# Transfers of x spaced in time, a token order of their own for the last two units, and new orders around 9-product jobs

## The chip, the cores and the metric

The kernel runs on one core of a Trainium2 chip. A core has five engines that run side by side, each its own instruction stream in order: TensorE (PE, matrix products; its weight loads are shown as PEld), VectorE (DVE), ScalarE (ACT), GpSimd (POOL) and SyncE (SP), which here issues nearly all DMA transfers. Products land in PSUM, eight banks of 128 x 512 float32 each, and have to be read out by VectorE or ScalarE before a bank can be written again. The metric is the device time of one execution in microseconds (us); the time before is the median of three runs.

## What is computed

The input x has 2048 rows of 512. Two branches are formed from it and mixed by a gate for each row:

```python
g = _sigmoid((x * gate_w).sum(-1, keepdims=True))
a = _A_ref(x, A_wq, A_wk, A_wv, A_wo)     # attention, 32 heads of 16, one shared key and value head
b = _B_ref(x, B_w_gate, B_w_up, B_w_down) # ((x W) * (x V)) W2, inner width 1792, no nonlinearity
return g * a + (1 - g) * b
```

The attention branch computes `scores = q k^T * 16^-0.5`, a softmax over the 2048 keys, and the weighted sum of the values, followed by the product with `wo`. All is float32 and stays accurate to it: a dense product of two float32 matrices is made of three products of their high and low parts (`mm3`, line 144).

## The kernel before

**Units and steps.** The queries are cut into 4 chunks `c` of 512 rows, 4 row tiles `t` of 128 in each, and 4 groups `g` of 8 heads. A unit is one (c, g, t): 64 units (line 107), each with 16 steps over the keys. For each step there are two products that give scores for the row maximum (`p1`, L705, tokens a and b, read by VectorE's maximum L706), two products that give the scores again with the maximum already subtracted (`p2`, L746, tokens c and d, read by ScalarE's exponential L747), and the products with the values (`pv`, L759; one token p is a round of 8 small products, two steps). The first kind runs 25 steps ahead (`LEAD`). When a unit's 16 steps of the first kind are done, `p1_end` (line 710) reduces the maxima, stores them to DRAM (`dm<-mt`, L726), and fetches them back as rows of the tile `Q` (`Q<-dm`, L733): the first product L746 of the unit can't start before these rows have landed.

**Lanes and fill.** The products a to f use 64 rows of the array each, and the two halves are two lanes: a, c, e on the one, b, d, f on the other; two products of different lanes run side by side. Tokens e and f are the fill: one product of 64 rows of the dense work of the FFN branch, of the projection to q and of the product with `wo` (L878). A `Job` is a chain of such products into one PSUM bank; the first lane runs 12 products ahead of the second, and when the second has done its last the bank is read out by the job's `evac`. A gate or up job has 12 products. For each group of FFN columns (`FGS`, of 3, 3, 4 and 4 columns of 128) four down jobs follow, one for each row tile, of 9 products (3 columns x 3) or 12. Four jobs of 9 fill the 36 fill tokens of exactly one unit, and such a unit has an order of its own.

**The written order.** PE's instructions stand in the order of strings of tokens: `ORDER` (144 tokens: 16 each of a to d, 36 each of e and f, 8 p) for a unit, `ORDER_NINE` for a unit with 9-product jobs, `ORDER_AFTER` for the unit behind it. The choice is made at the end of the function (line 971). There are 8 units of the second kind and 8 of the third. A planner that runs when the program is built (`State`, lines 408 to 482, and the dictionary `clock`) follows the order with assumed durations; it picks the PSUM bank for each product (`claim`), skips fill for which nothing is ready, and decides when DMA issues and the small work of the other engines are put into the streams: `later(ns, fn)` puts `fn` that many planned nanoseconds behind the present. Each stream keeps its order on the chip, so a late SP instruction holds back all that stand behind it in SP's stream.

**x.** The transposed x of a chunk, high and low part, is 8 tiles of 128 x 512 (256 KB each). At the start x of chunks 1 to 3 lies in tiles that the FFN uses later, and is stored to DRAM (`x_store`, L311: 24 transfers, planned from 35 us on, one each 1.2 us; the planner's zero lies at about 33 us of the span). When a chunk's FFN is done, `x_turn` loads the next chunk's x back (`x_load`, L198), all 8 transfers at once, and the next chunk's first job counts as ready 12 us later (`xat`).

**y.** Each output tile is the sum of five parts. `y_add` (line 350): ScalarE scales the first out of PSUM into y; for the others ScalarE scales the product out of PSUM into `yt` (L360) and GpSimd adds it (L361). Only in the tail, behind the last unit, VectorE does both in one instruction (L353). `st["idle"]` is true from the last product for the maxima (token a or b) on, about half way through the unit before the last; from there VectorE has little left to do. From there also, `claim` takes the bank that is free and was written last instead of the one that is free first, and tokens a and b serve as fill tokens.

Of the kernel before, what the change touches and what calls it, by code (L numbers as in the profile page):

```python
# [14 lines left out]
F32 = mybir.dt.float32  # L15
# [13 lines left out]
NJ = 16  # L29
# [9 lines left out]
GAP = 50.0  # L39
SEEN = 452.0  # L40
RED, RED_END = 602.0, 688.0
EXP, EXP_END = 490.0, 604.0
COPY, COPY_END = 505.0, 600.0
# [6 lines left out]
ORDER = (  # L50
    "cdefedafcfebefedafeedafcfedebefadebefcfefefebededebefadfefcfadeefebedcfa"
    "fcfcfafefefafafcfefafcfedcfafafefedebcfebefebebebcbppppcdadcbppdababcppb"
)
ORDER_NINE = (
    "cbedcefefafedafcffeadefedbeedfacfefafcfaffeebedbefcfedeebedaffcaffcfaeff"
    "faedfafcfcfeebcbcfededfebeeddappbcbcbappppbcabedeffedefecbefafefedebabpp"
)
ORDER_AFTER = (
    "adebcffefeadeebcfedebeffeadefadedaffefcfafeedbebecffeafcfaffcfedeaffcfeb"
    "cefefebabedcdpppcbcbadppcbdeebeffcebafedefedafcfefafcfebcfedefafedbapppb"  # L60
)
HALVES = (slice(0, 64), slice(64, 128))
KROWS = (slice(0, 48), slice(64, 112))
# [4 lines left out]
def mix_kernel(ctx: ExitStack, tc: tile.TileContext, x, wq, wk, wv, wo, wg, wu, wd, gw, out):  # L68
    nc = tc.nc
# [17 lines left out]
    def w512(tag, dt, bufs):  # L87
        return work.tile([128, 512], dt, name=tag, tag=tag, bufs=bufs)
# [26 lines left out]
    NS = NU * NJ  # L115
    clock = {"T": 0.0, "dve": 0.0, "act": 0.0, "pool": 0.0}
# [3 lines left out]
    def later(ns, fn):  # L120
        heapq.heappush(events, (clock["T"] + ns, next(serial), fn))
# [5 lines left out]
    def spend(eng, ns, after=0.0):  # L127
        clock[eng] = max(clock[eng], clock["T"], after) + ns
        return clock[eng]
# [29 lines left out]
    def ms_bank(i):  # L159
        return bank(i, f"ms{i}")  # L160
# [22 lines left out]
    st = {"gen": None, "next": None, "q": 0, "tail": False, "idle": False, "f": 0}  # L183

    xT = {}
    xd = {}

    def x_tiles(tags=None):
        if tags:
            return [[w512(tag, F32R, FG + 1) for _ in range(4)] for tag in tags]  # L190
        whole = [work.tile([128, 4, 512], F32R, name=tag, tag=tag, bufs=1) for tag in ("xh", "xl")]
        return [[w[:, k] for k in range(4)] for w in whole] + whole

    def x_load(c):
        xT[c] = x_tiles()
        for v in range(2):
            for k in range(4):
                nc.sync.dma_start(xT[c][v][k].bitcast(F32), xd[c][v * 4 + k])  # L198

    dq, dqat = {}, {}  # L200

    def at(t, fn):
        later(max(0.0, t - clock["T"]), fn)
# [143 lines left out]
    y = {}  # L347
    ydone = {}

    def y_add(c, t, p, gcol):  # L350
        end = spend("act", COPY)
        if st["tail"] and (c, t) in y:
            nc.vector.scalar_tensor_tensor(y[c, t], p, gcol, y[c, t], op0=OP.mult, op1=OP.add)  # L353
        elif (c, t) not in y:
            y[c, t] = w512("y", F32, 6)
            ydone[c, t] = 0
            nc.scalar.activation(y[c, t], p, AF.Copy, scale=gcol)
        else:
            tmp = w512("yt", F32, 2)
            nc.scalar.activation(tmp, p, AF.Copy, scale=gcol)  # L360
            nc.gpsimd.tensor_tensor(y[c, t], y[c, t], tmp, op=OP.add)  # L361
            end = spend("pool", 1240.0, end)
        ydone[c, t] += 1
        if ydone[c, t] == len(FGS) + 1:
            done = y.pop((c, t))
            at(end + 200.0, lambda: nc.sync.dma_start(out2[c * 512 + t * 128:c * 512 + t * 128 + 128, :], done))


    class Job:


        def __init__(self, prods, evac, ready, p=None, start=True):
            self.prods, self.evac, self.ready, self.p, self.start = prods, evac, ready, p, start
            self.end = self.items = self.bank = None
# [7 lines left out]
    def peek():  # L382
        if st["next"] is None and st["gen"] is not None:
            st["next"] = next(st["gen"], None)
            if st["next"] is None:
                st["gen"] = None
        if front and ready(front[0]) and (len(front) > 1 + (st["f"] > 9) and not st["tail"] or not ready(st["next"])):
            return front[0]
        return st["next"] if ready(st["next"]) else None

    def nine_unit():
        if nines and ready(nines[0][1][0]):
            group, group_jobs = nines.popleft()
            begun.add(group)
            nine.extend(group_jobs)
        return bool(nine)

    def take():
        if nine:
            return nine.popleft()  # L400
        j = peek()
        if front and j is front[0]:
            return front.popleft()
        st["next"] = None
        return j

    class State:
# [21 lines left out]

        def claim(self):  # L430
            b = self.free.index(min(self.free))
            if st["idle"] or self.npv == 0:
                b = max((i for i in range(NB) if self.free[i] <= max(min(self.nl), self.free[b])), key=lambda i: self.wrote[i])
            self.known = max(self.known, self.wrote[b])
            return b
# [42 lines left out]

    def evac(j, p):
        clock["act"] = max(clock["act"], clock["T"] + SEEN)  # L480
        j.evac(p)


# [7 lines left out]
    xat = {0: 0.0}  # L491
# [13 lines left out]

    def x_turn(c):
        x_load(c)
        xat[c] = clock["T"] + 12000.0

    order = [(c, f) for c in range(NC) for f in range(NF)]  # L510
    staged, W = {}, {}
# [296 lines left out]
    later(100.0, gate_sum)  # L808
    later(70000.0, gates)
    for i, f in enumerate(stores):  # L810
        later(35000.0 + 1200.0 * i, f)
    qat.update({0: 0.0, 1: 5000.0})
    st["gen"] = ffn_jobs()
    E = State()
# [10 lines left out]
    def fence():  # L825
        b = E.claim()
        p, t = bank(b, "fence"), work.tile([128, 32], F32, name="ft", bufs=2)
        for _ in range(2):
            nc.tensor.transpose(p[:32, :32], ident[:32, :32], ident[:32, :32])
            nc.vector.tensor_copy(t[0:32, :], p[:32, :32])  # L830
        E.seq += 1
        E.wrote[b] = E.known = E.seq
        E.nl = [max(E.nl) + 1000.0] * 2
        E.dve = max(E.dve, E.nl[0])
        E.free[b] = E.nl[0] + 300.0

    def fill(l):
        wait = 0.0
        if l == 0:
            if hole[0]:  # L840
                hole[0] -= 1
                run.append(None)
                pos[0] += 1
                return
            if not run or run[-1] is None or run[-1][1] + 1 == len(run[-1][0].items):
                for _ in range(40):
                    if nine or peek():
                        break
                    wait_ns(100.0)
                else:  # L850
                    hole[0] = 11
                    run.append(None)
                    pos[0] += 1
                    return
                j = take()
                j.items, j.bank = j.prods(), E.claim()
                wait, E.free[j.bank] = E.free[j.bank], 1e18
                j.p = ms_bank(j.bank)
                run.append((j, 0))
            else:  # L860
                run.append((run[-1][0], run[-1][1] + 1))
            j, i = run[-1]
        else:
            if run[pos[1]] is None:
                pos[1] += 1
                return
            j, i = run[pos[1]]
            if i == 0 and j.end > E.known:
                if E.npv:
                    late[0] += 1  # L870
                    return
                fence()
        pos[l] += 1
        at = E.issue(l, wait)
        E.wrote[j.bank] = E.seq
        lhs, rhs = j.items[i]
        end = i + 1 == len(j.items)
        nc.tensor.matmul(j.p, lhs[HALVES[l]], rhs[HALVES[l]], start=(l == 0 and i == 0), stop=(l == 1 and end))  # L878
        if end and l == 0:
            j.end = E.seq  # L880
        elif end:
            clock["T"], clock["act"] = max(clock["T"], at), max(E.act, at + SEEN)
            E.free[j.bank] = clock["act"] + COPY_END + GAP
            evac(j, j.p)
            E.act = max(E.act, clock["act"])

    def token(op):
        place(op)
        while late[0] and run[pos[1]][0].end <= E.known:
            late[0] -= 1  # L890
            fill(1)
# [32 lines left out]
    def wait_ns(ns):  # L924
        E.nl = [max(E.nl) + ns] * 2
        events_until(max(E.nl))
# [21 lines left out]
    while min(E.n1) < LEAD or pos[0] < FIRST[0] or pos[1] < FIRST[1]:  # L948
        l = 0 if E.nl[0] <= E.nl[1] else 1
        k = E.n1[l]  # L950
# [8 lines left out]
    is_nine = False  # L959
    while E.npv < NS:  # L960
        after, is_nine = is_nine, E.npv > 0 and not st["idle"] and nine_unit()
        for op in ORDER_NINE if is_nine else ORDER_AFTER if after else ORDER:
            token(op)
    events_until(max(E.nl))

# [9 lines left out]
    while events or front or st["gen"] or st["next"]:  # L975
        run_events()
        if peek():
            j = take()
# [28 lines left out]
```

## Time and profile before

| | |
|---|---|
| median of 3 runs | 1612.77 us (1607.96 to 1616.8) |
| the profiled execution: its own time | 1613.99 us |
| the profiled execution: span from first to last instruction | 1611.2 us |
| mean granted TensorE clock | 0.996 |
| PE busy | 1595.3 us, 99% |
| PE weight loads busy | 1039.4 us, 65% |
| DVE busy | 1360.5 us, 84% |
| ACT busy | 1205.8 us, 75% |
| POOL busy | 734.3 us, 46% |
| products for the maximum (L705), for the exponential (L746), with the values (L759), fill (L878) | 2048, 2048, 4096, 4752 |
| DMA | 121.44 MB, mean 75 GB/s |

The span and the run's own time differ by 2.8 us that lie outside the first and the last instruction. A busy PE is not a PE at its peak: products are pipelined, their recorded ends are modelled, and two lanes that are both busy look like one that is busy and one that is idle. So for PE the starts tell more than the busy share: how long a unit takes from one landmark in the order to the same landmark in the next. A landmark that is easy to find is the run of four rounds (`acc`, L759, x32) near the end of `ORDER`.

### The profile page before, as it was taken

How to read it: one execution, taken by the hardware profiler on the slowest of the kernel's cores; microseconds unless marked ns; L12 is line 12 of the kernel's file. 1: busy time of each engine (PE TensorE's matmuls, PEld its weight loads, DVE VectorE, ACT ScalarE, POOL GpSimd, SP SyncE). 2: the span in 40 equal slices, each digit the busy share in tenths (PEclk: the TensorE clock that was granted, in tenths of full speed). 3: DMA queues.
4: the chain of work that ended last, by engine and by line, in shares of the span. 5: the costliest groups of instructions: out<-in, count | busy, mean ns of one | idle time of the engine just before them, and what ended most of it. 6: DMA issues, size and time to landing. Idle time of an engine off the chain costs nothing.

```text
span 1611.2 us, 35399 instructions
## 1 busy us (share of the span) xinstructions
PE 1595.3 (99%) x13126; PEld 1039.4 (65%) x13126; DVE 1360.5 (84%) x2410; ACT 1205.8 (75%) x2380; POOL 734.3 (46%) x875
## 2 busy tenths in 40 slices
PE   9999999999999999999999999999999999999998
PEld 7766766665665666666666666576676666676665
DVE  6978988888988988888898888898878888888870
ACT  4667877787787777787787778787777777787785
POOL 5616636354534624454533635454442624554431
PEclk9999999999999999999999999999999999999999
DMA  5464322121232212121232212122232212221111
GB/s 162 159 212 130 98 65 70 46 69 54 67 105 77 73 48 73 55 73 54 59 110 67 76 54 74 50 70 67 61 94 65 73 54 75 59 64 52 33 30 40
DMA packets 184991, 121.44 MB, mean 75 GB/s; under 512 B 46196, under 2 KB 154356, under 8 KB 184820
## 3 DMA queue, kind: packets, MB, share of 16 engines
q1 hardware_dynamic: 183620, 118.87, 24.6%
q8 instruction: 103, 1.69, 0.4%
q14 instruction: 68, 0.56, 0.1%
q10 hardware_dynamic: 1200, 0.33, 0.1%
HBM read 82.96 MB, written 36.17 MB: 74 GB/s over the span
## 4 chain that ended last, share of the span: by engine, by line
PE 96%; DVE 1%; DMA 1%; SPq 0%; ACT 0%; issue 0%; POOL 0%; POOLq 0%; DVEq 0%
PE ms L878 32%; PE acc L759 28%; PE s L705 17%; PE s L746 17%; DVE mx L706 1%; PE ms L149 1%; DMA xl<-xd 0%; DMA Q<-dm 0%; DMA dq<-oh 0%; PE wo L149 0%; PE warm L770 0%; ACT P L747 0%; SPq L198 0%; SPq L726 0%; DMA dm<-mt 0%
## 5 line engine op out<-in xcount | busy, mean ns | idle before, releaser
L706 DVE TENSOR_REDUCE mx<-s 128x1 f32<-128x512 f32 x2048 | 1289.3, 685 | 186.9 <-PE s L705 108.6
L747 ACT ACTIVATE P<-s 128x512 f32<-128x512 f32 x2048 | 1061.5, 625 | 276.7 <-PE s L746 188.7
L746 PE MATMUL s<-Q,KK 50*128 50x512 f32 x2048 | 712.7, 410 | 7.0 <-DMA Q<-dm 6.7
L705 PE MATMUL s<-KK,Q 48*128 48x512 f32 x2048 | 708.0, 404 | 0.7 <-DMA Q<-dq 0.6
L759 PE MATMUL acc<-P,V 128*32 128x512 f32 x4096 | 479.6, 597 | 0.0
L746 PEld LDWEIGHTS s<-Q,KK 50*128 50x128 f32 x2048 | 358.7, 186 | 141.3 <-issue 53.8
L705 PEld LDWEIGHTS s<-KK,Q 48*128 48x128 f32 x2048 | 356.0, 186 | 102.6 <-issue 52.6
L878 PE MATMUL ms<-xh,wl 64*128 64x512 f32 x920 | 329.2, 393 | 0.0
L878 PE MATMUL ms<-xh,wh 64*128 64x512 f32 x920 | 326.1, 393 | 0.0
L878 PE MATMUL ms<-xl,wh 64*128 64x512 f32 x920 | 313.1, 392 | 0.0
L759 PEld LDWEIGHTS acc<-P,V 128*32 128x32 f32 x4096 | 117.9, 109 | 254.7 <-issue 223.3
L878 PEld LDWEIGHTS ms<-xh,wh 64*128 64x128 f32 x920 | 165.9, 186 | 15.1 <-issue 0.6
L361 POOL TENSOR_TENSOR y<-y,yt 128x512 f32<-128x512 f32 x63 | 81.2, 1288 | 204.6 <-ACT yt L360 204.6
L544 POOL TENSOR_TENSOR hf<-gs 128x512 f32<-128x512 f32 x56 | 72.1, 1287 | 220.7 <-ACT gs L533 220.6
L878 PEld LDWEIGHTS ms<-xh,wl 64*128 64x128 f32 x920 | 163.0, 186 | 8.7 <-issue 0.3
L878 PEld LDWEIGHTS ms<-xl,wh 64*128 64x128 f32 x920 | 156.1, 186 | 10.5
L878 PE MATMUL ms<-wdh,hl 64*128 64x512 f32 x448 | 162.6, 396 | 0.0
L878 PE MATMUL ms<-wdh,hh 64*128 64x512 f32 x448 | 162.1, 397 | 0.0
L641 POOL TENSOR_TENSOR oT<-raw,rb 128x128 f32<-128x128 f32 x63 | 28.9, 459 | 292.2 <-DMA rb<-dr 280.9
L878 PE MATMUL ms<-wdl,hh 64*128 64x512 f32 x448 | 161.1, 393 | 0.0
L137 POOL TENSOR_TENSOR wl<-wn,wh 128x512 fp32r<-128x512 f32 x116 | 149.3, 1287 | 9.3
L763 ACT COPY osb<-acc 128x512 f32<-128x512 f32 x64 | 37.5, 586 | 89.5 <-PE acc L759 83.2
(147 smaller groups left out, 1342.5 us busy)
## 6 DMA issues: line engine op xcount, KB each, us to landing
do<-osb SPq DMA_DIRECT2D x63, 256.0 KB
wn<-in_B_w_gate_dram SPq DMA_DIRECT2D x56, 256.0 KB
wn<-in_B_w_up_dram SPq DMA_DIRECT2D x56, 256.0 KB
wdn<-in_B_w_down_dram SPq DMA_DIRECT2D x56, 256.0 KB
Q<-dq SPq DMA_DIRECT2D x384, 32.0 KB
raw<-do SPq DMA_DIRECT2D x252, 32.0 KB
dq<-oh SPq DMA_DIRECT2D x16, 256.0 KB
dq<-ol SPq DMA_DIRECT2D x16, 256.0 KB
```

Of the source, the lines that this page charges most:

```text
L137: nc.gpsimd.tensor_tensor(lo, src, hi.bitcast(F32), op=OP.subtract)
L149: nc.tensor.matmul(p, l, r, start=start and i == 0, stop=stop and i == len(prods) - 1)
L361: nc.gpsimd.tensor_tensor(y[c, t], y[c, t], tmp, op=OP.add)
L544: nc.gpsimd.tensor_tensor(hf, gu[0], gu[1], op=OP.mult)
L641: nc.gpsimd.tensor_tensor(dst, raw[:, 0], rb, op=OP.mult)
L705: nc.tensor.matmul(p, q[r, slot], KK[r, kq * 512:(kq + 1) * 512], start=True, stop=True)
L706: nc.vector.tensor_reduce(mx[u][:, half * 4 + slot, kq:kq + 1], p, axis=AX.X, op=OP.max)
L746: nc.tensor.matmul(p, KK[r, j * 128:(j + 1) * 128], q[r].rearrange("p s q -> p (s q)"), start=True, stop=True)
L747: nc.scalar.activation(P[s][:, half], p, AF.Exp, scale=0.25)
L759: nc.tensor.matmul(acc[u][b:b + 32, :], V[:, j + i], src[:, half], start=(j == 0), stop=(j == NJ - 2))
L763: nc.scalar.copy(osb, acc.pop(u))
L878: nc.tensor.matmul(j.p, lhs[HALVES[l]], rhs[HALVES[l]], start=(l == 0 and i == 0), stop=(l == 1 and end))
```

## The change

It has five parts.

1. `x_load` puts its 8 transfers 2.5 us apart, and the job behind them counts as ready 23.5 us after the turn instead of 12. The 24 stores of `x_store` start at 8 us of the planner's time instead of 35, 2 us apart instead of 1.2.
2. The last two units are run from one string, `ORDER_LAST` (250 tokens: 7 each of a and b, 32 each of c and d, 72 e, 84 f, 16 p in runs of 5, 3, 3 and 5), instead of twice from `ORDER`.
3. From `st["idle"]` on, `y_add` uses VectorE's one instruction instead of ScalarE and GpSimd, and the planner counts the bank as free when VectorE is done.
4. `claim` takes the bank that is free first also after `st["idle"]`.
5. `ORDER_NINE` and `ORDER_AFTER` are new strings with the same counts of tokens. The rounds p stand in runs of 2, 2, 2, 2 in the first (2, 4, 2 before), and of 3, 2, 3 in the second (as before).

```diff
 ORDER_NINE = (
-    "cbedcefefafedafcffeadefedbeedfacfefafcfaffeebedbefcfedeebedaffcaffcfaeff"
-    "faedfafcfcfeebcbcfededfebeeddappbcbcbappppbcabedeffedefecbefafefedebabpp"
+    "cdebedefefafcbededeefebcfafcfefafcfefafbedefedafecfebefedabcffefefcfafef"
+    "afedafefcfebcfefccfebedadppadbadappadcdbappbcbeededefefcbefebcfefebabppf"
 )
 ORDER_AFTER = (
-    "adebcffefeadeebcfedebeffeadefadedaffefcfafeedbebecffeafcfaffcfedeaffcfeb"
-    "cefefebabedcdpppcbcbadppcbdeebeffcebafedefedafcfefafcfebcfedefafedbapppb"
+    "adefafcfebecffebefcebdedefaebedefafcfdefafeebedbedeafefdefedaefdebeedcfa"
+    "fcffeeffecffafefcebcfebcfafefdefafccfebfeadeffebcbapppdcbadcppbcbadapppb"
+)
+ORDER_LAST = (
+    "cdebefebefefedededebbcfefefebefedaefefefadcfefafcfefafefedadefebefedefcf"
+    "efcfafabefefedcffefcfefedccfeffcfedefcpppppdedcfefcfcfefefefedefeedcfefe"
+    "dfedcpppefedededeffefefededefedefefedcfcffcfefededdefefcfcffedfcfefefefe"
+    "fcfpppfcfcffcdfdfcfcdfffccfcfppppp"
 )
 def x_load(c):
         xT[c] = x_tiles()
-        for v in range(2):
-            for k in range(4):
-                nc.sync.dma_start(xT[c][v][k].bitcast(F32), xd[c][v * 4 + k])
+        for i in range(8):
+            later(2500.0 * i, lambda i=i: nc.sync.dma_start(xT[c][i // 4][i % 4].bitcast(F32), xd[c][i]))
 def y_add(c, t, p, gcol):
-        end = spend("act", COPY)
-        if st["tail"] and (c, t) in y:
+        end = spend("act", 0.0 if st["idle"] else COPY)
+        if st["idle"] and (c, t) in y:
+            end = spend("dve", 690.0)
             nc.vector.scalar_tensor_tensor(y[c, t], p, gcol, y[c, t], op0=OP.mult, op1=OP.add)
 def claim(self):
             b = self.free.index(min(self.free))
-            if st["idle"] or self.npv == 0:
+            if self.npv == 0:
 def evac(j, p):
         clock["act"] = max(clock["act"], clock["T"] + SEEN)
+        if st["idle"]:
+            clock["dve"] = max(clock["dve"], clock["T"] + SEEN)
 def x_turn(c):
         x_load(c)
-        xat[c] = clock["T"] + 12000.0
+        xat[c] = clock["T"] + 23500.0
     for i, f in enumerate(stores):
-        later(35000.0 + 1200.0 * i, f)
+        later(8000.0 + 2000.0 * i, f)
 def fill(l):
             evac(j, j.p)
-            E.act = max(E.act, clock["act"])
+            if st["idle"]:
+                E.free[j.bank] = max(E.dve, clock["dve"]) + 100.0 + GAP
+            E.act, E.dve = max(E.act, clock["act"]), max(E.dve, clock["dve"])
     while E.npv < NS:
         after, is_nine = is_nine, E.npv > 0 and not st["idle"] and nine_unit()
-        for op in ORDER_NINE if is_nine else ORDER_AFTER if after else ORDER:
+        last = E.npv == NS - 2 * NJ
+        for op in ORDER_LAST if last else ORDER_NINE if is_nine else ORDER_AFTER if after else ORDER:
             token(op)
```

## The prediction, made before the result was known

> **What bounds the kernel now.** The page comes first, for which engine the end hangs on.
>
> ```profile
> span 1611.2 us, 35399 instructions
> PE 1595.3 (99%) x13126; PEld 1039.4 (65%) x13126; DVE 1360.5 (84%) x2410; ACT 1205.8 (75%) x2380; POOL 734.3 (46%) x875
> ...
> PE 96%; DVE 1%; DMA 1%; SPq 0%; ACT 0%; issue 0%; POOL 0%; POOLq 0%; DVEq 0%
> ```
>
> TensorE carries 96% of the chain that ended last. All of its products stay, so only time that TensorE spends badly can be won. The busy share can't show that time (two lanes), so I read the chain in order of time for the landmark, the run of four rounds (x32) near the end of `ORDER`; the numbers are start and length in us.
>
> ```profile
> 51.00 8.38 DVE mx L706 x14
> 75.22 3.57 PE acc L759 x32
> 79.69 1.86 PE acc L759 x16
> ...
> 99.92 3.57 PE acc L759 x32
> 128.70 3.57 PE acc L759 x32
> ...
> 200.08 3.57 PE acc L759 x32
> ...
> 272.30 3.57 PE acc L759 x32
> ...
> 1132.52 3.60 PE acc L759 x32
> 1156.29 3.57 PE acc L759 x32
> ...
> 1181.91 6.21 DMA xl<-xd
> ...
> 1210.02 3.58 PE acc L759 x32
> ...
> 1377.38 3.57 PE acc L759 x32
> ...
> 1449.93 3.57 PE acc L759 x32
> ...
> 1544.97 3.57 PE acc L759 x32
> ...
> 1600.50 2.29 PE wo L149 x9
> ```
>
> A calm unit takes 1156.29 - 1132.52 = **23.77 us**. Against it stand four losses.
> - Unit 1: 99.92 - 75.22 = 24.70, **0.93** too long.
> - Unit 2: 128.70 - 99.92 = 28.78, **5.01** too long.
> - Around the last load of x: 1210.02 - 1156.29 = 53.73 for two units, **6.19** too long.
> - Each 9-product unit with the one behind it: from 200.08 to 272.30 lie three units, 72.22 against 71.31, **0.91** too long; the last of the eight such triples, 1377.38 to 1449.93, is 1.24 too long. A pair so takes about 72.22 - 23.77 = 48.45.
>
> What the first three wait for is told by the waits, SP's issues and the windows (PE, PEld, DVE, ACT and POOL busy, clock, DMA share, GB/s).
>
> ```profile
> PE s L746 <- DMA Q<-dm: 6.7, 3, 3.2
> ```
>
> ```profile
> 103.12 3.38 SPq L225 DMA_DIRECT2D Q<-dq  x6
> 106.60 2.68 SPq L726 DMA_DIRECT2D dm<-mt  x4
> ```
>
> ```profile
> 1156.62 1.29 SPq L726 DMA_DIRECT2D dm<-mt  x4
> ...
> 1158.87 0.54 SPq L733 DMA_DIRECT2D Q<-dm  x2
> ...
> 1178.69 1.76 SPq L198 DMA_DIRECT2D xh<-xd  x4
> 1180.55 1.80 SPq L198 DMA_DIRECT2D xl<-xd  x4
> 1182.39 4.15 SPq L225 DMA_DIRECT2D Q<-dq  x6
> 1187.26 2.10 SPq L726 DMA_DIRECT2D dm<-mt  x4
> ```
>
> ```profile
> 1191.05 1.62 DMA Q<-dm
> ```
>
> ```profile
> 100.00:105.00 5.00, 5.00 (x46) 1.57 (x44) 4.12 (x9) 1.59 (x4) 1.89 (x2) 1.00 0.95 311
> ```
>
> ```profile
> 1180.00:1185.00 5.00, 5.00 (x48) 1.66 (x50) 4.07 (x10) 1.51 (x3) 4.86 (x7) 1.00 0.92 302
> ...
> 1190.00:1195.00 5.00, 2.20 (x10) 2.23 (x12) 0.41 (x2) 1.40 (x3) 0.00 (x0) 0.65 0.54 161
> ```
>
> TensorE waits three times for the maxima's way through DRAM, at most 3.2 us. In a calm unit the store `dm<-mt` is issued at 1156.62; a period later that would be 1180.39, but it was issued at 1187.26, **6.87 late**, behind 8 loads of x and six fetches `Q<-dq` that themselves took 4.15 because the DMA engines were 92% busy. Unit 2 is the same with stores of x: `dm<-mt` went out at 106.60 behind fetches of 3.38, in a stretch of 95%. Its unit began 9.03 after the run at 99.92 (see 1553.97 below), at 108.95, 2.35 later; the calm store goes out 8.7 ahead of need (1156.29 + 9.0 - 1156.62). A wait of 3.2 us costs 6.19 because the granted clock falls to 0.65 behind it: the wait is half of the loss, the slow clock the other.
>
> **Part 1, transfers of x.** Nothing is removed: 24 loads and 24 stores of 256 KB remain, each an SP issue of 1.80 / 4 = 0.45. What changes is who stands behind them. At the last turn the `Q<-dq` and `dm<-mt` meet one load instead of eight: 0.45 of issue and 256 KB at the 302 GB/s of the full window, 0.87; 1.3 us. Calm slack: from 1156.62 to the end of the fetch's issue 2.8, landing 1.6 more (the chain's row at 1191.05), so 4.4 of 8.7; 4.3 are left. A store and a fetch that each meet a load use 2.6. The stall of 6.19 goes; I take **-6.1** (bounds 0 and -6.2). The job on the new x comes after four down jobs, 48 fill tokens, at 36 a unit 31.7 us, so readiness at 23.5 is hidden; the cover is 8 us. The other two turns lie in no stall and keep none by the same sum.
>
> The stores now run from 41 to 87 us of the span (33 + 8, then 46) instead of 68 to 96 and later. Unit 2 (maxima at about 100) is free of them: -5.0. Unit 1 still meets one at a time: 0.5 of its 0.93 stays. Together **-5.4** (bounds 0 and -5.9). In exchange, SP has stores ahead of unit 0's `dm<-mt` and of the fetches for units 2 and 3. Until 59.4 (51.00 + 8.38) the chain runs over VectorE's maxima, which hide a late first L746; unhidden it costs at most 2 x 1.3. I take **+0.3** (0 to +2.6), as the cover ends about when the first L746 is due.
>
> [...]
>
> **Part 5, the orders around 9-product jobs.** Slot and run lengths come from the rows.
>
> ```profile
> 1586.89 0.39 PE L878 MATMUL ms<-wdh,hh 64*128 64x512 f32 x1
> 1587.12 0.39 PE L878 MATMUL ms<-wdh,hl 64*128 64x512 f32 x1
> ```
>
> One lane starts a product each 0.23; a pair of different lanes shares a slot. A round is (3.57 - 1.86) / 2 = 0.855. `ORDER` has 136 products, 68 slots, 15.64, and 8 rounds, 6.84; what is left of 23.77, 1.29, belongs to three runs, 0.43 each. I counted slots in the strings, pairing neighbours of different lanes between runs: the old pair has 137 slots and 6 runs (31.51 + 13.68 + 2.58 = 47.77), the new one 136 slots and 7 runs (31.28 + 13.68 + 3.01 = 47.97). So the old pair's waits are 48.45 - 47.77 = 0.68, and the new string's bare length is 0.20 worse. What the waits are:
>
> ```profile
> PEld s L705 <- ACT P L747: 1.3, 4, 0.8
> PEld s L746 <- ACT P L747: 0.9, 4, 0.3
> PEld s L705 <- DVE mx L706: 0.8, 1, 0.8
> PEld s L746 <- DVE mx L706: 0.8, 1, 0.8
> ```
>
> In the window of the first pair TensorE's weight loads wait for banks that ScalarE and VectorE have still to read. If the new order frees all of it, a pair gains 0.48, eight 3.8; if none, it loses 0.20, eight +1.6. Shorter runs (2, 2, 2, 2) feed the readers more evenly, so I take half of the waits, 48.31: **-1.1** (bounds -3.8 and +1.6).
>
> **Parts 2 to 4, the last two units.**
>
> ```profile
> 1553.97 0.50 PE L705 MATMUL s<-KK,Q 48*128 48x512 f32 x1
> ```
>
> ```profile
> 1589.30 3.12 ACT L747 ACTIVATE P<-s 128x512 f32<-128x512 f32 x6
> ```
>
> ```profile
> L353 DVE SCALAR_TENSOR_TENSOR y<-wo,gg,y 128x512 f32<-128x512 f32 x1 | 0.8, 751 | 0.9 <-PE wo L149 0.9
> ```
>
> They last from 1553.97 to the last `wo` job at 1600.50, 46.53. The rows at 1586.89 and 1587.12 are successive starts of fill, 0.23 apart with the second lane empty: fill of one lane was used up early. `ORDER_LAST` has 72 e and 84 f, just what is left, 124 slots (28.52), 16 rounds (13.68) and 4 runs (1.72): 43.92. That is 2.61 less; 0.5 for waits gives **-2.1** (bounds -2.6 and +0.5). ScalarE's 64 exponentials at 3.12 / 6 = 0.52 are 33.3 of 43.9, so it can follow. The y sums that move to VectorE, at most five, cost 0.75 each on an engine that has no more maxima to take there; behind them in its stream wait only the reciprocals and the split for the last job. If that cover were gone it would be 3.8. `claim` alone I cost at nothing, since bank waits are in the 0.5.
>
> **Sum.** -6.1 - 5.4 + 0.3 - 1.1 - 2.1 = -14.4. The profiled run took 1613.99, 2.8 more than its span, so it would be 1599.6; it lies 1.2 over the median, so from the median I forecast **1598.4**.
>
> **Rivals.**
> - *The orders lose all waits.* For it: the waits are for banks alone. Against: the readers' load is unchanged. Pairs at -3.8, the last units at -2.6, unit 1 whole (-0.6 more): 1594.6.
> - *Banks hold the orders back.* ScalarE and VectorE empty banks no faster, so denser orders only move the waits: pairs +1.6, last units 0, 1603.2. For it: the four wait rows. Against: VectorE is busy 84%, ScalarE 75%. [...]
> - *The pacing doesn't pace.* SP's stream is in order; if it is held at another transfer's wait, the loads bunch again and one long stall stays: about +5, 1603.4. For it: SP took 4.15 over six fetches.
> - *Slower.* Loads of x now cover 20 us of each turn, and a unit sends maxima each 23.77 us, so nearly every turn has a `dm<-mt` among them, and so do units 0 and 1 with the stores. If one transfer ahead used up the slack, three turns would lose 6.2 each (+18.5 against the forecast) and two starts 5 each (+10): 1627. It decides where a met transfer costs over half of the 4.3 slack, 2.1; I found 1.3.
>
> **How the numbers follow.** Forecast 0.52, waits gone 0.16, banks 0.13, bunching 0.11, slower 0.04, rests 0.04. The range 1591 to 1606 holds the first four with the scatter of the runs. No change within 0.5% (about what a measurement of this kernel can tell) means over 1604.7: faster 0.83 (the first three and part of the fourth), same 0.13, slower 0.04.
>
> **What would show it.** Right: no unit over 24.5 us, clock 1.00 around both places, the `dm<-mt` behind the last turn issued about 8 us ahead of its unit; pairs near 48.3; 44.4 from the last two units' begin to the `wo` job. Wrong: an `xd` transfer in the chain, a wait of L746 for `Q<-dm` at units 0 or 1, or pairs above 48.6.

## The result, and the profile after

The changed kernel takes **1595.85 us** (median of 4 runs, 1594.36 to 1597.38) against 1612.65 (median of 4, 1607.96 to 1616.8): a ratio of **0.9897, 95% interval 0.9868 to 0.9926**, 16.8 us. The forecast was 1598.4 with 1591 to 1606. The profiled execution took 1595.37 us with a span of 1593.6, 17.6 less than before.

First the page of the changed kernel, then its chain of work in order of time (start and length in us); `pv` stands at L767 here, `p2` at L754, `p1` at L713.

```profile
span 1593.6 us, 35423 instructions
PE 1585.4 (99%) x13126; PEld 1038.5 (65%) x13126; DVE 1364.3 (86%) x2415; ACT 1200.9 (75%) x2375; POOL 728.2 (46%) x870
...
PE 98%; DVE 1%; issue 0%; ACT 0%; POOL 0%; POOLq 0%
```

```profile
74.82 3.57 PE acc L767 x32
98.55 3.57 PE acc L767 x32
122.33 3.57 PE acc L767 x32
146.50 3.57 PE acc L767 x32
...
193.99 3.57 PE acc L767 x32
...
265.83 3.57 PE acc L767 x32
...
1148.32 3.57 PE acc L767 x32
1172.05 3.57 PE acc L767 x32
1195.89 3.59 PE acc L767 x32
```

DMA has left the chain's shares. The same landmark as before tells where the time went: units 1 and 2 take 98.55 - 74.82 = 23.73 and 23.78 (24.70 and 28.78 before), unit 3 takes 24.17; the last turn of x lies between 1148.32 and 1195.89, two units of 23.73 and 23.84; and the triple with the first 9-product pair takes 71.84 instead of 72.22.

A unit's length can also be taken from the first product behind the last round of the unit before to the first product behind its own last round, as at 1553.97 in the prediction; all lengths below are made so. Over the whole span:

| place | before | changed | difference |
|---|---|---|---|
| end of the first unit | 84.23 | 83.82 | -0.4 |
| unit 1 | 24.71 | 23.75 | -1.0 |
| unit 2 | 28.75 | 23.76 | -5.0 |
| unit 3 | 23.86 | 24.17 | +0.3 |
| eight 9-product pairs, mean of one | 48.47 | 48.08 | -3.1 in all |
| unit 47 (last turn of x) | 29.97 | 23.87 | -6.1 |
| last two units | 46.46 | 43.86 | -2.6 |
| from there to the end | 10.75 | 10.94 | +0.2 |

The other 41 units together are 974.72 and 974.74 us: nothing moved in them. The table sums to -17.7 with its rounding.

SP's stream around the last turn, of the changed kernel:

```profile
1170.72 0.33 SPq L203 DMA_DIRECT2D xh<-xd  x1
1171.10 2.77 SPq L230 DMA_DIRECT2D Q<-dq  x6
1173.97 1.29 SPq L734 DMA_DIRECT2D dm<-mt  x4
...
1175.81 2.23 SPq L203 DMA_DIRECT2D xh<-xd  x2
...
1178.69 0.57 SPq L741 DMA_DIRECT2D Q<-dm  x2
```

One load instead of eight stands ahead of the store of the maxima. The six fetches take 2.77 instead of 4.15, and `dm<-mt` goes out 7.1 us ahead of the unit's first product at 1181.07, where it had gone out 1.8 ahead of the unit's begin. Between store and fetch lie 4.7 us; two paced loads, held up together, are issued in between. So the cover that is left is thin: 2.4 us from the fetch's issue to need, of which 1.6 were the landing in the prediction's row. The rows also show what the pacing is: an order in SP's stream, not a time. The eight loads, planned 2.5 us apart, go out one at 1170.72, two from 1175.81 on, and so on.

### The profile page after: what moved, and what is told of

Same layout as the page of the kernel before. It is cut to its first block, busy times and chain, and to the rows that moved or that the text cites. A ratio compares the mean times of both kernels' runs of the same rounds, so it can differ in the third digit from the quotient of the medians.

```text
span 1593.6 us, 35423 instructions
## 1 busy us (share of the span) xinstructions
PE 1585.4 (99%) x13126; PEld 1038.5 (65%) x13126; DVE 1364.3 (86%) x2415; ACT 1200.9 (75%) x2375; POOL 728.2 (46%) x870
## 4 chain that ended last, share of the span: by engine, by line
PE 98%; DVE 1%; issue 0%; ACT 0%; POOL 0%; POOLq 0%
PE ms L886 33%; PE acc L767 29%; PE s L754 17%; PE s L713 17%; DVE mx L714 1%; PE ms L155 1%; PE px L279 0%; PE warm L778 0%; PE wo L155 0%; PE pick L686 0%; PE pv L308 0%; PE px L266 0%; DVE y L359 0%; DVE KK L302 0%; ACT KK L301 0%
## 5 line engine op out<-in xcount | busy, mean ns | idle before, releaser
L754 PE MATMUL s<-Q,KK 50*128 50x512 f32 x2048 | 705.0, 407 | 0.0
L713 PE MATMUL s<-KK,Q 48*128 48x512 f32 x2048 | 700.8, 401 | 0.3 <-DVE KK L302 0.2
L767 PE MATMUL acc<-P,V 128*32 128x512 f32 x4096 | 480.5, 597 | 0.0
L754 PEld LDWEIGHTS s<-Q,KK 50*128 50x128 f32 x2048 | 355.9, 185 | 119.5 <-ACT P L755 40.8
L713 PEld LDWEIGHTS s<-KK,Q 48*128 48x128 f32 x2048 | 352.4, 185 | 106.0 <-issue 52.8
L767 PEld LDWEIGHTS acc<-P,V 128*32 128x32 f32 x4096 | 116.9, 109 | 254.6 <-issue 222.4
L367 POOL TENSOR_TENSOR y<-y,yt 128x512 f32<-128x512 f32 x58 | 74.7, 1288 | 212.2 <-ACT yt L366 197.7
L886 PE MATMUL ms<-wdh,hl 64*128 64x512 f32 x448 | 158.3, 393 | 0.0
L886 PE MATMUL ms<-wdl,hh 64*128 64x512 f32 x448 | 155.5, 394 | 0.0
L886 PE MATMUL ms<-wdh,hh 64*128 64x512 f32 x448 | 155.5, 393 | 0.0
```

What stands on the lines that cost most here:

```text
L713: nc.tensor.matmul(p, q[r, slot], KK[r, kq * 512:(kq + 1) * 512], start=True, stop=True)
L754: nc.tensor.matmul(p, KK[r, j * 128:(j + 1) * 128], q[r].rearrange("p s q -> p (s q)"), start=True, stop=True)
L767: nc.tensor.matmul(acc[u][b:b + 32, :], V[:, j + i], src[:, half], start=(j == 0), stop=(j == NJ - 2))
```

## The experiments

My theory was that each part works at its own place and that the parts add; for the long stalls, that the small transfers of the maxima stand behind the large ones of x, so that their place against each other decides. The rivals: that the parts only moved each other in time, that eight loads at once always cost, that the orders gain nothing since the banks are emptied no faster.

### Each part alone, on the kernel before

The paced loads:

```diff
-        for v in range(2):
-            for k in range(4):
-                nc.sync.dma_start(xT[c][v][k].bitcast(F32), xd[c][v * 4 + k])
+        for i in range(8):
+            later(2500.0 * i, lambda i=i: nc.sync.dma_start(xT[c][i // 4][i % 4].bitcast(F32), xd[c][i]))
-        xat[c] = clock["T"] + 12000.0
+        xat[c] = clock["T"] + 23500.0
```

> The kernel before with the paced loads of x alone (2.5 us apart, ready after 23.5). Theory that each part works at its own place: the unit that took 29.97 us takes 23.8 to 23.9, -6.1; units 1 and 2 keep 24.7 and 28.8; all other units within 0.1 of before; time about 1606.6. Rival, that the stall went because the other parts moved the maxima against the loads: the unit still takes over 28, time about 1612.

The early stores:

```diff
-        later(35000.0 + 1200.0 * i, f)
+        later(8000.0 + 2000.0 * i, f)
```

> The kernel before with the early stores of x alone. Theory of own places: unit 1 falls from 24.7 to 23.8, unit 2 from 28.8 to 23.8, unit 3 gains 0.3, the first unit ends about 0.4 earlier; -6.0 in all by unit 3, the stall of 6.2 at the last load of x stays; time about 1606.7. Rival, that stores in the first unit hold back its own maxima: the first unit ends over 0.5 later.

The two strings around 9-product jobs:

```diff
-ORDER_NINE = (...)
-ORDER_AFTER = (...)
+ORDER_NINE = (...)
+ORDER_AFTER = (...)
```

> The kernel before with the new strings for 9-product jobs alone. Theory of own places: each of the eight pairs takes 48.0 to 48.1 instead of 48.4, -3.0 in all; the stalls at units 1, 2 and 47 stay; time about 1609.7. Rival, that the gain of the pairs came from the other parts: pairs stay at 48.4, time about 1612.7.

The parts of the last two units:

```diff
+        last = E.npv == NS - 2 * NJ
-        for op in ORDER_NINE if is_nine else ORDER_AFTER if after else ORDER:
+        for op in ORDER_LAST if last else ORDER_NINE if is_nine else ORDER_AFTER if after else ORDER:
...
-            if st["idle"] or self.npv == 0:
+            if self.npv == 0:
...
-        if st["tail"] and (c, t) in y:
+        if st["idle"] and (c, t) in y:
```

> The kernel before with the parts of the last two units alone (the string, y added by VectorE there, claim, the planner's clock). Theory of own places: the last two units take 43.9 instead of 46.5, -2.6, nothing else moves; time about 1610. Rival, that the last units gain because they are reached earlier with more work landed: under 1 us.

Lengths in us, and the time of the one run (the kernel before took 1616.2 on that chip). Single runs of the kernel before lie between 1607.44 and 1617.44, so the lengths carry the argument and the times don't:

| | before | x_paced | stores_early | nine_orders | last_units |
|---|---|---|---|---|---|
| first unit ends | 84.23 | 83.75 | 86.30 | 84.75 | 87.37 |
| unit 1 | 24.71 | 24.11 | **23.75** | 24.48 | 24.24 |
| unit 2 | 28.75 | 28.54 | **23.78** | 26.61 | 26.66 |
| unit 47 | 29.97 | **23.82** | 29.86 | 29.13 | 29.90 |
| pair, mean | 48.47 | 48.47 | 48.47 | **48.08** | 48.46 |
| last two | 46.46 | 46.40 | 46.41 | 47.16 | **43.86** |
| time | | 1605.82 | 1609.0 | 1608.03 | 1610.58 |

Each part gains at its own place what it gained in the whole. Units 1 and 2 vary by up to 2.1 also where no edit touches them (nine_orders, last_units); the last section tells a part of why. So the rival that they only shift each other falls, with one exception: with the new strings for the pairs alone, the last two units take 0.7 longer than before, by the old `ORDER`. Why was not followed up, since `ORDER_LAST` takes their place.

The row for the first unit holds a miss. With early stores it ended 2.1 us later than before, which looks like the rival I had named. What TensorE waited for near the start, in that run and then in the run of the last units alone, whose start is that of the kernel before:

```profile
PE s L705 <- DMA Q<-dq: 1.7, 1, 1.7
```

```profile
PE s L714 <- DMA Q<-dq: 1.3, 1, 1.3
```

In both, TensorE waited for the first fetch of q, about 24 us into the span and ahead of any store of x (the first goes out at 26.43, behind these fetches in SP's stream), and the first unit ended at 86.30 and 87.37. Such a wait is 0.6 in the trace of before, so it explains a part of the 2.1, and the same code without early stores can be later still. Another part is the granted clock. In the run with early stores it is 0.50 for 3.41 us about 61 us into the span (the row has PE, PEld, DVE, ACT and POOL busy, clock, DMA share, GB/s):

```profile
61.30:64.71 3.41, 3.41 (x18) 2.71 (x18) 3.29 (x6) 2.60 (x7) 2.55 (x3) 0.50 0.23 62
```

Nine of the thirteen traces have such a stretch near 60 us, four of the six with late stores and five of the seven with early ones. In the nine the first unit ends at 84.63 to 87.37 (the latest, last_units, has a second one, at 24.62), in the four without at 84.23 and 83.75 (late stores) and 83.82 and 83.73 (early stores). Over all traces, with the stores late it ended at 83.75 to 87.37 (six traces, mean 84.99), with the stores early at 83.73 to 86.30 (seven traces, mean 84.66). A cost of the early stores in the first unit does not show, and the start scatters by some 3 us in either kernel.

### Eight loads at once, placed against the maxima

Both on the changed kernel, with the first line of `x_load`'s loop replaced. First placed to miss:

```diff
-            later(2500.0 * i, lambda i=i: nc.sync.dma_start(...))
+            later({1: 0.0, 2: 0.0, 3: 8000.0}[c], lambda i=i: nc.sync.dma_start(...))
```

> The changed kernel, but each turn's eight loads of x are issued at once again; those of the last turn 8 us later than the turn, so that they stand behind the unit's store and fetch of the maxima. Theory that the place against the maxima decides: no stall, unit 47 takes 23.8 to 24.0 and units 17 and 32 23.8, time as the changed kernel, about 1596. Rival, that eight at once always cost and only the spacing helps: one of the three units takes over 27.

Then placed to hit:

```diff
+            later({1: 8200.0, 2: 6800.0, 3: 0.0}[c], lambda i=i: nc.sync.dma_start(...))
```

> The changed kernel with eight loads at once, placed against the maxima: in the first turn 8.2 us after the turn, 1.6 us ahead of the maxima as the last turn of the kernel before had it; in the second 6.8 us after, 1.7 us behind the maxima, between their store and their fetch; in the last 0. Theory of the place: unit 17 and unit 47 take 29 to 30 each, with the clock at 0.6 to 0.7 for some 6 us behind the wait; unit 32 waits less, 1 to 3 us, and if its wait stays under about 2.5 the clock stays at 1.00 and the unit loses only the wait itself; time 1607 to 1611. Rival, that the stall belongs to the last turn alone: units 17 and 32 stay at 23.8, time about 1602.

| | changed | missing | hits |
|---|---|---|---|
| unit 17 (first turn) | 23.84 | 23.83 | 25.20 |
| unit 32 (second turn) | 23.82 | 24.87 | 25.29 |
| unit 47 (last turn) | 23.87 | 23.82 | 29.04 |
| time | 1595.85 | 1595.86 | 1603.99 |

SP's stream of the run that was placed to miss, around the last turn:

```profile
1169.81 2.86 SPq L230 DMA_DIRECT2D Q<-dq  x6
1172.93 1.59 SPq L734 DMA_DIRECT2D dm<-mt  x4
...
1176.56 0.56 SPq L741 DMA_DIRECT2D Q<-dm  x2
...
1179.44 1.93 SPq L203 DMA_DIRECT2D xh<-xd  x4
1181.47 2.08 SPq L203 DMA_DIRECT2D xl<-xd  x4
```

Eight loads at once, behind the fetch of the maxima, cost unit 47 nothing. So for the 6.1 us the place decides and not the spacing; the spacing made a place harmless that was not. In the second turn, left where it was, the burst now cost 1.05, since the store of the maxima went out 3.9 us late behind it, where it had been 2.8 in the trace of before.

In the run placed to hit all three turns lose time, so the rival that the stall belongs to the last turn falls. Unit 32 came as expected: a wait of about 1, the clock at 1.00, and 1.5 lost. But my size for unit 17 was wrong: I expected 29 to 30 and measured 25.20 (and so 1603.99 in all, not 1607 to 1611). The burst began 3.1 us ahead of the maxima there and not 1.6 (454.46 against 457.60, where the store goes out in a calm unit), and `dm<-mt` was 5.4 us late instead of 6.4 as in unit 47. Its fetch also followed sooner, 3.2 us behind the store (466.16) instead of 4.2. Two microseconds of lateness so separate a wait of about 1 from one of 3.3. The next rows are the list of waits and the windows of the waits and of what follows them.

```profile
PE s L754 <- DMA Q<-dm: 5.3, 3, 3.3
```

```profile
466.00:468.00 2.00, 1.07 (x7) 0.46 (x5) 1.32 (x3) 0.59 (x1) 0.00 (x0) 1.00 0.06 6
468.00:470.00 2.00, 2.00 (x19) 1.99 (x20) 1.04 (x2) 1.68 (x4) 0.76 (x2) 1.00 0.50 172
...
1185.00:1190.00 5.00, 1.72 (x10) 1.69 (x11) 0.69 (x1) 1.41 (x4) 0.00 (x0) 0.87 0.42 117
1190.00:1195.00 5.00, 5.00 (x37) 4.82 (x35) 4.07 (x7) 3.91 (x8) 0.46 (x1) 0.79 0.23 72
```

Of the three waits, 5.3 in all, the longest was 3.3 and the others about 1 each. Behind the wait at 466 the clock stays at 1.00 and the unit loses 1.4; behind the one at 1185 it falls to 0.87 and 0.79, and the unit loses 5.3; in the 3.41 us from 1188.71 on it is 0.50.

### One of the two strings, and the pieces of the last units

> The kernel before with the new ORDER_NINE and the old ORDER_AFTER. Theory that each string has its own waits: the first unit of a pair takes 24.1 instead of 24.4, the second stays at 24.05, pairs 48.15. Rival, that the second unit pays for the first's order: the second over 24.2 and the pair at 48.4 or more.

With the new `ORDER_NINE` and the old `ORDER_AFTER` the first unit of a pair falls by 0.3 (24.40 to 24.09 in unit 6), but the second rises by 0.1 to 0.2 (24.10 to 24.23 in unit 7); the mean pair is 48.32, between 48.47 and 48.08. The expectation of independent strings missed: the second pays about half back, short of the rival's 48.4, and it takes the new `ORDER_AFTER` to get the rest.

> The kernel before with ORDER_LAST alone; y is added by ScalarE and GpSimd and claim is as before. Theory that the string is what gains: the last two units take 44 to 44.6 instead of 46.5 (VectorE's y and claim give the rest to 43.86). Rival, that ScalarE can't follow with the y work on it: 45.2 or more.

The string alone, on the kernel before, brings the last two units to 44.50, three quarters of the 2.6. For the next two runs, first the changed kernel with the old `claim`:

```diff
-            if self.npv == 0:
+            if st["idle"] or self.npv == 0:
```

> The changed kernel with the old claim (after the last maxima the bank written last is taken again). ORDER_LAST alone gave 44.50 us for the last two units, all parts 43.86; 0.64 belong to claim and VectorE's y. Theory that VectorE's y carries them, since ScalarE is what the banks wait for: 43.9 to 44.0 here. Rival, that the choice of banks carries them: 44.3 or more.

And the changed kernel with `y_add`, `evac` and `fill` as before:

```diff
-        end = spend("act", 0.0 if st["idle"] else COPY)
-        if st["idle"] and (c, t) in y:
-            end = spend("dve", 690.0)
+        end = spend("act", COPY)
+        if st["tail"] and (c, t) in y:
...
```

> The changed kernel with y of the last two units added by ScalarE and GpSimd again. Theory that VectorE's y carries the 0.64 us: the last two units take 44.3 to 44.5. Rival, the choice of banks: 43.9 to 44.0.

The old `claim` gives 44.21, ScalarE's y 44.88. Both expectations missed: each piece is worth more than I gave it, 0.35 and 1.02, and together more than the 0.64 that both bring over the string alone. The new `claim` with y on ScalarE is worse than the old one with it (44.88 against 44.50), so the pieces don't add: here the other choice of banks paid only where ScalarE was relieved. The landmark hides a part of this. Of the 156 fill products 151 lie ahead of it with the new `claim` and 155 with the old one; the others run behind it. From the same begin to the end of the span it is 54.80 for the changed kernel, 55.37 with the old `claim`, 55.79 with ScalarE's y, 55.68 for the string alone and 57.21 before. Counted so, the string alone brings 1.5 of 2.4, and with ScalarE's y the two choices of banks differ by 0.1 only. The windows of the last two units show the relief, first of the changed kernel, then with ScalarE's y:

```profile
1538.75:1582.60 43.85, 43.85 (x362) 28.85 (x358) 14.93 (x28) 34.48 (x68) 6.64 (x10) 1.00 0.13 41
```

```profile
1539.40:1584.30 44.90, 44.82 (x363) 28.58 (x359) 11.95 (x24) 36.68 (x72) 11.63 (x14) 1.00 0.13 40
```

ScalarE is busy 2.2 us less (four instructions fewer), VectorE 3.0 more, out of a window of 44. The times of these runs, one each, were 1611.69 (the new `ORDER_NINE` alone), 1610.01 (the string alone), 1596.74 (old `claim`) and 1596.97 (ScalarE's y).

### Another bank for `pick`, the last unit's division

Rows near the end of the changed kernel, then one more edit, and the same rows with it:

```profile
1583.63 0.39 PE L886 MATMUL ms<-wdl,hh 64*128 64x512 f32 x1
1584.05 0.75 DVE L359 SCALAR_TENSOR_TENSOR y<-ms,gb,y 128x512 f32<-128x512 f32 x1 [6.63 <-PE ms L886]
...
1584.95 2.02 PE L686 MATMUL pick<-osb,wn 128*128 128x128 f32 x16 [0.94 <-DVE y L359]
```

```diff
-            p = bank(3 + (E.accb == 3), "pick")
+            b = min((i for i in range(NB) if i not in (E.accb, st["pb"])), key=lambda i: E.free[i])
+            p = bank(b, "pick")
```

(`st["pb"]` is the number of the bank `wo`.)

> The changed kernel with one more edit: the products of the last unit's division (pick) take the bank that is free first, instead of bank 3 or 4. In the changed kernel they waited 0.94 us for VectorE's y of the last down job, which lies in the same bank; in the run of the last units alone they did not, and the time from the last round to the end was 9.99 instead of 10.94. Theory that this wait sets the end: 9.9 to 10.1 from the last round to the end, median 0.9 us under the changed kernel, about 1594.9. Rival, that the chain behind it hides the wait: 10.8 to 11.0.

```profile
1584.06 0.39 PE L888 MATMUL ms<-wdl,hh 64*128 64x512 f32 x1
1584.37 2.05 PE L688 MATMUL pick<-osb,wn 128*128 128x128 f32 x16
1584.48 0.75 DVE L359 SCALAR_TENSOR_TENSOR y<-ms,gb,y 128x512 f32<-128x512 f32 x1 [6.60 <-PE ms L888]
```

The products no longer wait for VectorE's y, and from the last round to the end it is 9.98 instead of 10.94: the wait set the end. The median of four runs was 1595.34 (1594.8 to 1595.53; ratio to the kernel before 0.9903, 0.9886 to 0.992). The expected 0.9 under the changed kernel didn't show in the median: the two are 0.5 us apart, in runs that were not made side by side. That it gains rests on the trace.

## Why the prediction was right, and where it was off

The forecast of -14.4 met -16.8. By its terms, predicted and measured in the traces:

- **Loads of x, -6.1: -6.1.** The step held, and the two other turns stayed calm as said. The cover was thinner than my sum: I allowed 2.6 us for two met loads out of 4.3. The store went out 7.1 ahead of its unit instead of 8.7, and the fetch 4.7 behind the store instead of 2.25, where SP held two paced loads together. That is 4.1 of the 4.3, so the full gain was met with little to spare.
- **Stores of x, -5.4: -6.0** for units 1 and 2. I kept 0.5 of unit 1's loss for stores that it still meets; it lost nothing. The stores also ran otherwise than I worked out: three went out together at 26.0 to 27.0, the next at 46.5, the last at 85.4, where I had 41 to 87. And the size leans on one trace: in the six traces with late stores units 1 and 2 lose 3.4 to 5.9 together, 4.6 as a mean, in the seven with early stores nothing over 0.1. Unit 3 gave 0.3 back in the changed kernel: its first product L754 started 0.42 behind the product before it (131.33, 131.75), as the fetches of the maxima landed (the second at 131.80). Three of the seven traces with early stores have such a wait, of 0.42 to 0.49; the early stores alone don't, so it is not shown to be theirs.
- **The start, +0.3: -0.4,** within a scatter of 3 us of the same instructions. Where the clock stayed at 1.00 through the first unit, early and late stores lie within 0.5 of each other, two traces each.
- **The pairs, -1.1: -3.1.** This is the term that was mis-sized. The step "I take half of the waits" failed: the new pair takes 48.08, 0.11 over the bare length that I counted, where the old one was 0.7 over. The price of a run, 0.43, and the waits may both be off. Nor are the weight loads' waits the measure that I took them for. In the first pair of the changed kernel they are

```profile
PEld s L713 <- ACT P L755: 2.7, 4, 0.8
...
PEld s L754 <- DVE mx L714: 0.8, 1, 0.8
PEld acc L767 <- ACT P L755: 0.6, 2, 0.3
PEld s L754 <- ACT P L755: 0.2, 1, 0.2
```

  4.3 us, about as long as in the old pair (4.5, of which the prediction shows 3.8), and yet the pair is 0.4 shorter. So why the new strings lose less stays open: that shorter runs feed the readers more evenly was not tested apart from the rest of the strings, and how far my 0.43 for a run was too much isn't known.
- **The last two units, -2.1: -2.6.** The count of slots, rounds and runs gave 43.92 and the trace 43.86; the 0.5 that I had set aside for waits did not come there. The match is in part luck: paired as in the count of the pairs, the string has 123 slots and not 124 (43.69), and five products of the second lane were left over and ran behind the last round. There `pick` also waited 0.94 for VectorE's y, and 0.2 were given back. My mark of 44.4 to the `wo` job can't be read any more, since that job now runs behind `pick`, from 1586.72 on. VectorE's y was not free, as I had costed it: here it stood in front of `pick`. And `claim`, which I costed at nothing, is worth 0.35 (0.57 to the end of the span).

Of the rivals, "the orders lose all waits" came nearest in its terms (-3.8 and -2.6 against -3.1 and -2.6) and in its sum, 1594.6. "Banks hold the orders back" fell: the pairs gained with ScalarE at 75% and VectorE at 86%, so neither engine was the limit of a whole unit. "The pacing doesn't pace" was seen in small (two loads issued together at 1175.81, three stores at 26.0) and didn't decide. "Slower" was tested in part, by the run placed to hit: with time lost in all three turns the changed kernel took 1604, still under the kernel before.

## What to carry to other kernels

When a small transfer with a deadline shares a queue with large ones, place the large ones against it, or space them so that the place matters less (unit 47 took 29.04 us with eight loads ahead of the store of the maxima, 23.82 with them behind the fetch, 23.87 with them spaced), and look at the cover that is left; the gain is at one spot and can be read from one landmark in a written order. Count what an order must take at least (slots, rounds, runs) and compare it with the measured period: here the new pair came within 0.11 us of its count, while the sum of an engine's waits was no measure of the loss (4.3 us of them against 4.5, and the pair 0.4 shorter). Work moved to an idle engine still needs its bank and its place in the stream looked at, down to the last instruction: VectorE's y held `pick` up by 0.94.

## What the runs showed of the hardware that I had not expected

The waits of TensorE for the maxima had two prices in these traces. Each gives a pair: the time from the start of the last product to the first of the new unit, and what the unit lost against 23.78.

| start to start, us | loss, us | traces |
|---|---|---|
| 0.42 to 1.54 | 0.33 to 1.51 (never more than 0.11 from the first column) | 12 waits |
| 2.80, 2.85, 3.17 | 2.88, 2.83, 3.10 | last_units, nine_orders, last_string_only, unit 2 |
| 3.29, 3.51, 3.71 | 4.76, 4.97, 5.18 | x_paced, before, nine_string_only, unit 2 |
| 3.53 to 4.07 | 5.26 to 6.19 | 7 waits, unit 47 |

The units of the waits up to 3.17 lost the wait and no more; those of the waits from 3.29 on lost 1.5 to 2.6 us on top. The granted clock shows what came on top: behind each of these ten waits it was 0.50, for 3.41 us in seven (1.46 to 1.50 on top) and for 6.83 in three (unit 47 of before, stores_early and last_units: 2.35 to 2.55). Rows of the trace of before, then of last_string_only, in the columns of the windows above:

```profile
1191.48:1198.31 6.83, 5.51 (x26) 5.54 (x28) 2.09 (x4) 3.18 (x6) 0.46 (x1) 0.50 0.37 108
```

```profile
107.41:110.82 3.41, 2.14 (x17) 0.53 (x9) 2.63 (x5) 1.10 (x3) 0.00 (x0) 1.00 0.29 99
110.82:114.24 3.42, 2.02 (x17) 2.05 (x19) 0.81 (x2) 1.46 (x4) 0.00 (x0) 1.00 0.40 137
...
1189.44:1192.85 3.41, 1.70 (x14) 1.73 (x16) 0.50 (x1) 1.20 (x3) 0.00 (x0) 1.00 0.57 163
1192.85:1196.26 3.41, 3.41 (x19) 3.41 (x17) 2.21 (x4) 2.67 (x6) 0.46 (x1) 0.50 0.25 83
```

The first two rows of last_string_only hold its wait of 3.17, with the clock at 1.00 in both and no drop behind them; the last two hold the end of its wait in unit 47 and what follows, with the clock at 0.50 in the second. The length of a wait alone was not shown to decide: the gap in the table between 3.17 and 3.29 is only where the waits of these traces lie. In stores_early the clock was 0.50 from 61.30 on (the row further up), and its list of waits has none of a product of TensorE between 30 and 90 us. What decides when the clock falls is not shown.

So the twelve waits up to 1.54 cost their own length, as the three of 2.80 to 3.17 did, and the ten from 3.29 to 4.07 cost 1.46 to 2.55 more. A part of the old kernel's scatter lies there: in the six traces with late stores unit 2 took 28.54 to 28.96 in the three with a drop behind its wait, and 26.61 to 26.88 in the three without.
